# Re-measured durations in a kernel's instruction planner, and the order of all instructions searched anew

## The chip, the cores and the metric

The kernel runs on one core of a Trainium2 chip. The metric is the time of one execution on the device, in microseconds (us). Five engines work side by side, each through its own queue in order: PE (TensorE: matmuls and transposes, with its weight loads shown apart as PEld), DVE (VectorE), ACT (ScalarE), POOL (GpSimd) and SP (SyncE, which here only issues DMAs).

## What is computed

Two stages on a batch of 4, 8 heads, 768 steps and 48 channels per head, all in float32. The first is a recurrence per head:

```python
for t in range(S):
    cur = np.einsum('bhd,bhe->bhde', u[None] * kt, vt)
    y[:, :, t] = np.einsum('bhd,bhde->bhe', rt, state + cur)
    state = wt[:, :, :, None] * state + np.einsum('bhd,bhe->bhde', kt, vt)
```

The second takes y as x (4 x 768 x 384) through four attention experts of width 64. A gate picks two experts for each token; each expert is causal attention:

```python
    q = x @ wq[e];  k = x @ wk[e];  v = x @ wv[e]
    scores = scale * (q @ k.transpose(0, 2, 1))      # causal mask, then softmax
    ye = a @ v @ wo[e]
    out += mask[..., None] * w[:, :, kk:kk + 1] * ye   # the two picked experts
```

## The kernel before

The work is cut into 8 units (b, g): batch b, and half g of the sequence (384 steps). Each unit has a recurrence part, `rwkv`, and an attention part, `moe`, which needs the x of its own unit and, for g = 1, the K and V of both halves.

In `rwkv` the recurrence is done in chunks of 64 steps, six to a unit, for four pairs of heads p. The names in the rows are those of its tiles, and the digits behind a name are batch, half and pair. Two scans on DVE make the running products of the decay within each chunk, `suf` (L377) and `pre` (L381). Four elementwise products may stand on DVE or on POOL, as the planner chooses: `kt` (k by suf, L384), `mr` (r by pre, written over `pre`, L386), `uk` and `ur` (written over `nat`, L391 and L394). `rk` (L397) is a sum on DVE, `ux` (`xn`: for each head three small instructions on ACT, L404, or one on DVE or POOL, L406) starts the tile of y. PE transposes the keys (`ktp`, L414), makes the chunks' states (`ups`, L431), the products within a chunk (`aps`, L493, for two pairs at once) and the two parts of y (`yps`, L469 and L472). DVE carries the state from chunk to chunk by five or six instructions that depend on each other (`wst`, L440); a state scaled by the decay is `ys` (L450, DVE or POOL). DVE masks `aps` into `am` (L502) and adds `yps` to `xn` (L478). PE transposes y (`xp`, L519), ACT and DVE split it into a high and a low part (`xh` L521, `xl` L523).

In `moe` PE projects (`pp` L565 for Q and K, `vp` L588 for V and the gate), makes the scores (`sp`, L656 and L661), transposes the weights of the softmax (`tp`, L686), multiplies them by V (`yp`, L714) and projects out (`op`, L782). DVE finds each row's maximum (`mx`, L670), ACT takes the exponential (`a`, L672), and the copies out of PSUM (`ATa`, `ATb`, `kts`, `ob`, `v_sb`) stand on ACT (L226) or DVE (L228). Two banks of PSUM serve `rwkv` (`rw`), two `moe` (`mo`), and two double ones the scores (`sc`).

Nothing of the order is written by hand. `Plan.add` records each piece of work with its reads and writes, the engines that it may run on and its duration on each. `Plan.order` then plays the program through: at each step it takes, over all engines, the piece that could start first. On one engine it chooses among the pieces that could start within a slack of 125 ns by a due time, which is the stage's due time plus the entry of the table `WISH` for this kind of work and this unit. A change of PE's tiling costs `DRAIN`, a wait for another engine costs the entry of `WAITS`, and pieces in `BOTH` do not run on DVE and POOL at once. What comes out is the order of each engine's queue, the choice of engine and the buffer of each tile. The chip then runs these queues with semaphores; the planned times themselves are used nowhere.

PE's queue also holds 94 matmuls that compute nothing (`warm`, L832): 14 come first, and 80 are due last of all, so that they fill holes at the start.

## Time and profile before

| what | us |
|---|---|
| median of 3 runs (377.25 to 378.18) | 377.8 |
| the profiled execution | 380.95 |
| its span, first to last instruction | 379.2 |
| PE busy | 358.2 |
| DVE busy | 318.4 |
| ACT busy | 203.8 |
| POOL busy | 145.7 |

A row of the timeline gives start and duration of one instruction, or of several of a kind in a row, from the span's start. Matmuls overlap: on PE the start-to-start distance is the cost. An instruction's duration on the other engines also overlaps the next one's by a tenth of a microsecond where they don't depend on each other.

### The profile page before, as it was taken

What the parts mean: (1) busy time and instruction counts of PE and PEld (TensorE: products, weight loads), DVE (VectorE), ACT (ScalarE), POOL (GpSimd) and SP (SyncE); (2) the same over time, 40 slices, a digit from 0 to 9 for tenths busy, and PEclk for the clock granted to TensorE, in tenths of its full rate; (3) what the DMA queues carried; (4) which work ended last, traced back from release to release, by engine and by line L of the source; (5) the groups of instructions that cost most, each with busy time, mean ns of one, the idle gap of its engine ahead of it and who ended that gap; (6) DMA issues with size and microseconds to landing.
All of it is one profiled execution on the core that took longest, in us unless ns stands there. A gap on an engine that the chain in (4) does not pass through costs nothing.

```text
span 379.2 us, 12634 instructions
## 1 busy us (share of the span) xinstructions
PE 358.2 (94%) x5123; PEld 274.8 (72%) x5131; DVE 318.4 (84%) x800; ACT 203.8 (54%) x601; POOL 145.7 (38%) x262
## 2 busy tenths in 40 slices
PE   7889989999999999998899999999999999999996
PEld 2445777688867777776786867787887769977865
DVE  6999997988999999849997999997999965366863
ACT  3262325746666646736643654637764733376663
POOL 2758453735611536132571555833622010210010
PEclk9999999999999999999999999999999999999999
DMA  7877525353525354423374335454203001000101
GB/s 257 330 255 257 176 94 162 99 184 117 170 72 182 104 149 131 141 63 100 128 211 131 110 96 174 144 174 142 67 16 111 3 18 45 22 2 2 42 22 63
DMA packets 18058, 45.17 MB, mean 119 GB/s; under 512 B 2000, under 2 KB 9424, under 8 KB 18000
## 3 DMA queue, kind: packets, MB, share of 16 engines
q1 hardware_dynamic: 18000, 44.37, 36.1%
q8 instruction: 40, 0.66, 0.8%
q14 instruction: 18, 0.15, 0.1%
HBM read 39.64 MB, written 4.72 MB: 117 GB/s over the span
## 4 chain that ended last, share of the span: by engine, by line
PE 58%; DVE 25%; ACT 5%; issue 4%; DMA 2%; POOL 2%; ACTq 0%; DVEq 0%; POOLq 0%; SPq 0%
PE pp L565 9%; PE yp L714 8%; PE tp L686 8%; PE sp L656 7%; PE vp L588 5%; DVE mx L670 5%; PE op L782 5%; DVE wst L440 4%; DVE suf L377 3%; DVE am L502 3%; PE yps L472 3%; ACT a L672 3%; PE ups L431 2%; DMA nat<-in_nat_dram 2%; DVE pre L381 2%
## 5 line engine op out<-in xcount | busy, mean ns | idle before, releaser
L672 ACT ACTIVATE a<-sp,mx 128x128 f32<-128x128 f32 (+5 forms) x96 | 60.6, 635 | 32.1 <-DVE mx L670 31.2
L670 DVE TENSOR_REDUCE mx<-sp 128x1 f32<-128x128 f32 (+5 forms) x96 | 56.8, 617 | 6.9 <-PE sp L661 5.2
L686 PE MATMUL tp<-ident,a 128*128 128x128 f32 x336 | 56.5, 285 | 4.0 <-ACT a L672 1.6
L686 PEld LDWEIGHTS tp<-ident,a 128*128 128x128 f32 x336 | 37.0, 140 | 15.8 <-ACT a L672 5.1
L440 DVE SCALAR_TENSOR_TENSOR wst<-wst,suf,ups 112x48 f32<-112x48 f32 x160 | 41.5, 260 | 5.3 <-PE ups L431 1.2
L226 ACT COPY ATa<-tp 128x512 f32<-128x512 f32 (+3 forms) x70 | 33.6, 493 | 17.3 <-PE tp L686 16.8
L377 DVE TENSOR_TENSOR_SCAN suf<-lt,one_suf 128x390 f32<-128x390 f32 x32 | 34.4, 1076 | 3.5 <-DMA lt<-in_wkr_dram 1.7
L714 PE MATMUL yp<-ATa,v_sb 128*64 128x384 f32 (+2 forms) x240 | 37.2, 433 | 0.2 <-ACT ATa L226 0.2
L565 PE MATMUL pp<-xh,wh_qk 128*128 128x384 f32 x96 | 36.9, 384 | 0.2
L404 ACT ACTIVATE xn<-nat,rk 128x48 f32<-128x48 f32 x108 | 27.4, 324 | 17.5 <-DVE rk L397 17.4
L386 POOL TENSOR_TENSOR pre<-lt,pre 128x384 f32<-128x384 f32 x22 | 22.9, 1042 | 30.8 <-DVE pre L381 30.8
L450 POOL TENSOR_TENSOR ys<-wst,suf 112x240 f32<-112x240 f32 (+1 forms) x27 | 21.3, 790 | 34.5 <-DVE wst L440 20.7
L381 DVE TENSOR_TENSOR_SCAN pre<-lt,inv_pre 128x390 f32<-128x390 f32 x32 | 32.9, 1027 | 0.4
L565 PE MATMUL pp<-xh,wl_qk 128*128 128x384 f32 x96 | 32.7, 341 | 0.0
L565 PE MATMUL pp<-xl,wh_qk 128*128 128x384 f32 x96 | 32.7, 340 | 0.0
L472 PEld LDWEIGHTS yps<-ys,pre 64*64 64x64 f32 (+1 forms) x704 | 23.3, 136 | 12.7 <-issue 6.8
L472 PE MATMUL yps<-ys,pre 64*64 64x48 f32 (+1 forms) x704 | 28.2, 225 | 4.1 <-DVE am L502 1.8
L394 POOL TENSOR_TENSOR nat<-nat 128x288 f32<-128x288 f32 x28 | 24.2, 868 | 14.2 <-DVE nat L391 11.3
L391 POOL TENSOR_TENSOR nat<-nat,u_sb 128x288 f32<-128x288 f32 x23 | 21.4, 932 | 20.5 <-DMA nat<-in_nat_dram 11.8
L384 POOL TENSOR_TENSOR kt<-lt,suf 128x384 f32<-128x384 f32 x22 | 21.1, 961 | 20.2 <-DVE suf L377 15.9
L469 PE MATMUL yps<-vy,am 64*64 64x48 f32 x768 | 27.5, 223 | 0.0
L502 DVE TENSOR_TENSOR am<-aps,dec_mask 64x384 f32<-64x384 f32 (+1 forms) x48 | 26.4, 549 | 0.9
(129 smaller groups left out, 869.7 us busy)
## 6 DMA issues: line engine op xcount, KB each, us to landing
lt<-in_wkr_dram SPq DMA_DIRECT2D x31, 579.5 KB, 4.3
nat<-in_nat_dram SPq DMA_DIRECT2D x32, 432.0 KB, 3.5
vy<-in_vY_dram SPq DMA_DIRECT2D x32, 144.0 KB, 2.6
out_dram<-ob SPq DMA_DIRECT2D x24, 192.0 KB, 1.9
...
```

Source lines behind the costliest of these rows:

```text
L226: nc.scalar.copy(o, i)
L377: plan.add("suf", {"DVE": t_scan(WB)}, lambda e, suf=suf, w_=w_: nc.vector.tensor_tensor_scan(rev(suf()), rev(w_()), rev(one_suf), 0.0, op ...
L381: plan.add("pre", {"DVE": t_scan(WB)}, lambda e, pre=pre, w_=w_: nc.vector.tensor_tensor_scan(flat(pre()), w_()[:, 0:WB - 1], flat(inv_pre ...
L440: nc.vector.scalar_tensor_tensor(new, ws[0:112, c0 + c - 1, :], sfv()[0:112, c, 0:1], u()[0:112, o], op0=ALU.mult, op1=ALU.add)
L469: nc.tensor.matmul(yps[h]()[half(q), o], am()[half(h), c, :], vy()[half(h), c, :], start=zero, stop=i == 2)
L472: nc.tensor.matmul(yps[h]()[half(q), o], pre()[r, c, 0:C], ys()[r, c, :], start=i == 0, stop=False)
L502: nc.vector.tensor_tensor(am()[o], aps()[i, 0:NH * C].rearrange("p (c j) -> p c j", j=C), dec_mask[i, None, :].to_broadcast([i.stop - i.st ...
L565: nc.tensor.matmul(pp()[:, 0:384], w[:, qk, k, cs], x()[:, k, :], start=(k == j == 0), stop=(k == j == 2))
L670: plan.add("max", {"DVE": t_dve(n)}, lambda e, x=x, mx=mx: nc.vector.tensor_reduce(mx(), spv(x), axis=AX.XY, op=ALU.max, negate=True), [sp ...
L672: plan.add("exp", {"ACT": t_exp(n)}, lambda e, x=x, y=y, mx=mx, a=a: nc.scalar.activation(a()[:, 0:n].rearrange("p (a n) -> p a n", a=np_) ...
L686: nc.tensor.transpose(tp()[:, j * 128:(j + 1) * 128], a()[:, (j0 + j) * 128:(j0 + j + 1) * 128], ident)
L714: nc.tensor.matmul(yp()[e * 64:e * 64 + 64, lo:hi], v_sb[ep]()[:, j, e * 64:e * 64 + 64], at, start=(j == 0), stop=(j == nj - 1))
```

## The change

Durations that the planner is told are replaced, and the table of due times is a new one, found by searching anew with these durations. No arithmetic, no tile, no size and no number of buffers changes. The planner also looks at 40 instead of 24 candidates of each engine, and `ys`, which may stand on DVE or POOL before and now, costs 100 ns more on DVE. The rows of `WISH` (58 kinds of work by 8 units) are new but for entries that no work uses; two are shown.

```diff
 def t_pool(cols):
-    return 30 + 2.45 * cols
+    return 60 + 2.25 * cols
...
-         "ACT": dict(PE=164 + SAFE, DVE=143, ACT=127, POOL=170, SP=130), ...
+         "ACT": dict(PE=185 + SAFE, DVE=180, ACT=127, POOL=170, SP=130), ...
...
-    def order(self, free, slack=60.0, width=24):
+    def order(self, free, slack=60.0, width=40):
...
-                    plan.add("ws", {"DVE": 115}, grow, ...
+                    plan.add("ws", {"DVE": 172}, grow, ...
...
-            plan.add("ys", prod((NH - 1 + g) * D), scaled, ...
+            plan.add("ys", {"DVE": t_dve((NH - 1 + g) * D) + 100, "POOL": t_pool((NH - 1 + g) * D)}, scaled, ...
...
-                    plan.add("am", {"DVE": t_dve(384)}, mask, [apss[x]], [(am, h)])
+                    plan.add("am", {"DVE": 575 if x == 0 else 565}, mask, [apss[x]], [(am, h)])
...
-                plan.add("proj", {"PE": 3 * 172}, mm, ...
+                plan.add("proj", {"PE": 525}, mm, ...
...
-                plan.add("vproj", {"PE": 3 * 122}, mm, ...
+                plan.add("vproj", {"PE": 356}, mm, ...
...
-                plan.add("av", {"PE": 2 * 0.905 * (hi - lo) + 4}, mm,
+                plan.add("av", {"PE": 1.68 * (hi - lo) + 2}, mm,
...
-            plan.add("g3", {"DVE": 640}, over, ...
+            plan.add("g3", {"DVE": 530}, over, ...
...
-                plan.add("op", {"PE": 3 * 172}, mm, ...
+                plan.add("op", {"PE": 522}, mm, ...
...
-    am=[-523.53, -400.44, -469.75, -522.32, -432.29, -446.5, -350.6, -400.44],
+    am=[-301.84, -35.43, -160.17, -6.95, -164.62, -115.51, -12.82, -195.52],
...
-    uk=[-496.59, -240.01, 105.83, -310.53, -51.05, -237.91, 134.69, -17.82],
+    uk=[392.44, 446.59, 355.21, 364.53, 378.87, 449.7, 367.72, 367.15],
...
-T_APS, T_UPS, T_YPS = 1100, (395, 330), (816, 890)
-DRAIN = 100
-T_SC = (330, 500, 670, 850, 1040, 1210)
+T_APS, T_UPS, T_YPS = 763, (393, 380), (737, 750)
+DRAIN = 95
+T_SC = (490, 562, 745, 915, 1085, 1275)
```

Counted in the two programs: PE has the same matmuls in both, and changes its tiling 261 times before and 262 times now. All 94 `warm` stand ahead of the first projection (`pp0000`) in both. DVE has 24 instructions fewer, POOL 10 more and ACT 24 more:

| work | DVE before, now | POOL before, now | ACT before, now |
|---|---|---|---|
| `kt` | 10, 5 | 22, 27 | |
| `mr` (`pre`) | 10, 6 | 22, 26 | |
| `uk` (`nat`, L391) | 9, 2 | 23, 30 | |
| `ur` (`nat`, L394) | 4, 6 | 28, 26 | |
| `ys` | 5, 3 | 27, 29 | |
| `ux` (`xn`; three small ones on ACT stand for one of the others) | 10, 11 | 18, 12 | 108, 123 |
| copies `ATa` | 26, 15 | | 70, 81 |
| copies `ATb`, `kts`, `ob` | 14, 9, 5 before; 13, 8, 3 now | | 18, 23, 19 before; 19, 24, 21 now |
| copies `v_sb` | 1, 7 | | 47, 41 |

The first place is in the recurrence of unit (0, 1), while unit (0, 0) is projected. DVE's queue before, from the end of one state's chain (`wst`) to the mask `am` of the pairs 0 and 1, for which PE's `yps010` waits:

```order
L440 SCALAR_TENSOR_TENSOR wst1_81<-wst1_81,suf011_649,ups0110_740 112x48
L594 COPY lg00_775<-vp001_756 128x4
L377 SCALAR_TENSOR_TENSOR suf012_791<-lt012_483,one_suf_66 128x390
L377 SCALAR_TENSOR_TENSOR suf013_821<-lt013_510,one_suf_66 128x390
L502 TENSOR_TENSOR am010_830<-aps010_795,dec_mask_86 128x384
L502 TENSOR_TENSOR am011_836<-aps011_797,dec_mask_86 64x384 x2
```

And now:

```order
L577 TENSOR_TENSOR Kl00_775<-pp0001_729,Kh00_767 128x384
L440 SCALAR_TENSOR_TENSOR wst1_81<-wst1_81,suf011_584,ups0110_738 112x48
L440 SCALAR_TENSOR_TENSOR wst1_81<-wst1_81,suf011_584,ups0111_741 112x48
L440 SCALAR_TENSOR_TENSOR wst1_81<-wst1_81,suf011_584,ups0110_738 112x48
L381 SCALAR_TENSOR_TENSOR pre012_791<-lt012_404,inv_pre_69 128x390
L572 SCALAR_TENSOR_TENSOR Ql001_821<-pp0010_763,Qh001_788 128x384
L502 TENSOR_TENSOR am010_827<-aps010_795,dec_mask_86 128x384
L502 TENSOR_TENSOR am011_833<-aps011_797,dec_mask_86 64x384 x2
L577 TENSOR_TENSOR Kl01_854<-pp0011_784,Kh01_839 128x384
L397 TENSOR_REDUCE rk013_860<-nat013_720 128x6
L377 SCALAR_TENSOR_TENSOR suf013_895<-lt013_419,one_suf_66 128x390
```

The scan `suf013`, which stood directly ahead of the masks, now stands behind them; the scan `pre012` and a split of Q stand ahead.

POOL's queue at the same place before:

```order
L450 TENSOR_TENSOR ys010_738<-wst0_80,suf010_508 112x288
L394 TENSOR_TENSOR nat013_714<-nat013_714 128x288
L450 TENSOR_TENSOR ys011_793<-wst1_81,suf011_649 112x288
L384 TENSOR_TENSOR kt012_832<-lt012_483,suf012_791 128x384
L384 TENSOR_TENSOR kt013_842<-lt013_510,suf013_821 128x384
```

And now (`ys010` is on DVE):

```order
L391 TENSOR_TENSOR nat013_720<-nat013_720,u_sb_84 128x288
L384 TENSOR_TENSOR kt012_780<-lt012_404,suf012_761 128x384
L450 TENSOR_TENSOR ys011_793<-wst1_81,suf011_584 112x288
L394 TENSOR_TENSOR nat013_720<-nat013_720 128x288
L386 TENSOR_TENSOR pre012_791<-lt012_404,pre012_791 128x6x64
L391 TENSOR_TENSOR nat100_755<-nat100_755,u_sb_84 128x288
L394 TENSOR_TENSOR nat100_755<-nat100_755 128x288
L384 TENSOR_TENSOR kt013_913<-lt013_419,suf013_895 128x384
```

Between `kt012` and `kt013` POOL now has five other products.

The second place is in the recurrence of unit (2, 0). DVE's queue before, around the chain `wst2`, whose reads free the PSUM banks that PE's `yps201` then writes:

```order
L377 SCALAR_TENSOR_TENSOR suf203_3262<-lt203_2684,one_suf_66 128x390
L440 SCALAR_TENSOR_TENSOR wst2_82<-wst2_82,suf202_3101,ups2021_3248 112x48
L391 TENSOR_TENSOR nat210_3214<-nat210_3214,u_sb_84 128x288
L440 SCALAR_TENSOR_TENSOR wst2_82<-wst2_82,suf202_3101,ups2020_3245 112x48
L228 COPY ATb1101_3305<-tp11114_3279 128x128
L440 SCALAR_TENSOR_TENSOR wst2_82<-wst2_82,suf202_3101,ups2021_3248 112x48
L379 RECIPROCAL inv_pre_69<-suf203_3262 128x6
L440 SCALAR_TENSOR_TENSOR wst2_82<-wst2_82,suf202_3101,ups2020_3245 112x48
L440 SCALAR_TENSOR_TENSOR wst2_82<-wst2_82,suf202_3101,ups2021_3248 112x48
```

And now:

```order
L478 TENSOR_TENSOR xn20_2485<-yps2010_3204,xn20_2485 128x3x48
L478 TENSOR_TENSOR xn20_2485<-yps2011_3206,xn20_2485 128x3x48
L228 COPY wst2_82<-ups2020_3248 112x48
L440 SCALAR_TENSOR_TENSOR wst2_82<-wst2_82,suf202_2922,ups2021_3251 112x48
L440 SCALAR_TENSOR_TENSOR wst2_82<-wst2_82,suf202_2922,ups2020_3248 112x48
L440 SCALAR_TENSOR_TENSOR wst2_82<-wst2_82,suf202_2922,ups2021_3251 112x48
L440 SCALAR_TENSOR_TENSOR wst2_82<-wst2_82,suf202_2922,ups2020_3248 112x48
L440 SCALAR_TENSOR_TENSOR wst2_82<-wst2_82,suf202_2922,ups2021_3251 112x48
```

The chain now stands behind the additions of `yps201`, without other work inside it. Over the whole program a `wst` directly follows another one 80 times now and 70 times before, of 160.

## Rows read from the trace of the kernel before

**Rows 1.** Busy time of each engine over the span, its share, and its instructions (the page's first part).

```profile
PE 358.2 (94%) x5123; PEld 274.8 (72%) x5131; DVE 318.4 (84%) x800; ACT 203.8 (54%) x601; POOL 145.7 (38%) x262
```

**Rows 2.** Busy time by stage: the stretch, its length, then busy time and instructions of PE, PEld, DVE, ACT and POOL, PE's granted clock, the DMA engines' share and GB/s.

```profile
0.00:42.00 42.00, 35.65 (x480) 18.78 (x489) 36.86 (x86) 15.92 (x48) 23.89 (x37) 1.00 0.74 260
42.00:60.00 18.00, 16.35 (x253) 14.43 (x251) 15.58 (x41) 4.56 (x16) 10.04 (x16) 0.91 0.40 129
60.00:300.00 240.00, 230.56 (x3522) 181.52 (x3522) 217.84 (x554) 140.99 (x421) 103.79 (x173) 1.00 0.40 125
300.00:360.00 60.00, 59.88 (x736) 48.38 (x735) 38.99 (x99) 32.53 (x94) 6.28 (x27) 1.00 0.06 21
360.00:379.20 19.20, 15.74 (x140) 11.73 (x138) 9.16 (x24) 9.80 (x24) 1.71 (x9) 1.00 0.12 42
```

**Rows 3.** The same by stage for the instructions on the tile `warm` alone: PE's busy time and instructions.

```profile
0.00:42.00 42.00, 24.57 (x86) 1.00 0.74 260
```

**Rows 4.** Pieces of the chain of work that ended last, in order of time: start, length, engine, tile, line and number of matmuls.

```profile
83.22 0.86 PE aps L493 x48
...
162.93 3.17 PE pp L565 x18
...
292.45 3.38 PE yp L714 x24
...
322.49 4.33 PE vp L588 x36
```

**Rows 5.** The timeline at the first place, of PE, DVE and POOL: start, duration, engine, line, operation, tiles, shape; in brackets the engine's idle time before it and what ended it.

```profile
48.51 0.96 DVE L377 TENSOR_TENSOR_SCAN suf<-lt,one_suf 128x390 f32<-128x390 f32 x1
48.60 1.34 POOL L450 TENSOR_TENSOR ys<-wst,suf 112x288 f32<-112x288 f32 x1
48.66 0.93 PE L493 MATMUL aps<-pre,kt 64*64 64x64 f32 x48
...
49.90 0.96 POOL L384 TENSOR_TENSOR kt<-lt,suf 128x384 f32<-128x384 f32 x1
49.97 1.72 DVE L377 TENSOR_TENSOR_SCAN suf<-lt,one_suf 128x390 f32<-128x390 f32 x1 [0.51 <-POOL ys L450]
...
51.38 0.34 PE L565 MATMUL pp<-xl,wh_qk 128*128 128x384 f32 x1
51.61 1.68 DVE L502 TENSOR_TENSOR am<-aps,dec_mask 128x384 f32<-128x384 f32 x3
...
52.28 0.32 PE L472 MATMUL yps<-ys,pre 64*64 64x48 f32 x4 [0.56 <-DVE am L502]
...
53.44 0.26 PE L472 MATMUL yps<-ys,pre 48*64 48x48 f32 x2 [0.83 <-DVE am L502]
```

**Rows 6.** The timeline at the second place, of DVE, POOL and PE.

```profile
182.26 0.24 DVE L440 SCALAR_TENSOR_TENSOR wst<-wst,suf,ups 112x48 f32<-112x48 f32 x1
182.49 1.23 DVE L391 TENSOR_TENSOR nat<-nat,u_sb 128x288 f32<-128x288 f32 x1
...
184.30 0.57 DVE L440 SCALAR_TENSOR_TENSOR wst<-wst,suf,ups 112x48 f32<-112x48 f32 x2
...
182.43 0.98 POOL L384 TENSOR_TENSOR kt<-lt,suf 128x384 f32<-128x384 f32 x1 [1.08 <-DVE suf L377]
...
183.37 0.29 PE L661 MATMUL sp<-causal,idh 64*128 64x128 bf16 x4
184.71 0.28 PE L472 MATMUL yps<-ys,pre 64*64 64x48 f32 x2 [1.06 <-POOL nat L394]
```

**Rows 7.** Groups of instructions of work that changes its engine: line, engine, operation, tiles, shape, number, busy time, mean ns of one, then idle time of the engine before them.

```profile
L384 DVE TENSOR_TENSOR kt<-lt,suf 128x384 f32<-128x384 f32 x10 | 6.4, 644 | 0.1
L386 DVE TENSOR_TENSOR pre<-lt,pre 128x384 f32<-128x384 f32 x10 | 6.2, 616 | 0.1
L391 DVE TENSOR_TENSOR nat<-nat,u_sb 128x288 f32<-128x288 f32 x9 | 6.0, 664 | 0.5 <-DMA nat<-in_nat_dram 0.5
L450 DVE TENSOR_TENSOR ys<-wst,suf 112x288 f32<-112x288 f32 (+1 forms) x5 | 2.2, 446 | 0.1
L228 DVE COPY ATa<-tp 128x512 f32<-128x512 f32 (+3 forms) x26 | 13.0, 510 | 4.5 <-PE tp L686 4.2
L394 DVE TENSOR_TENSOR nat<-nat 128x288 f32<-128x288 f32 x4 | 2.4, 602 | 0.0
L228 DVE COPY v_sb<-vp 128x128 f32<-128x128 f32 x1 | 0.3, 280 | 0.0
L384 POOL TENSOR_TENSOR kt<-lt,suf 128x384 f32<-128x384 f32 x22 | 21.1, 961 | 20.2 <-DVE suf L377 15.9 <-PE tp L686 4.2
L391 POOL TENSOR_TENSOR nat<-nat,u_sb 128x288 f32<-128x288 f32 x23 | 21.4, 932 | 20.5 <-DMA nat<-in_nat_dram 11.8 <-ACT ATa L226 7.7 <-PE sp L661 0.5
```

**Rows 8.** The same for the two scans and the chain of states, which stay on DVE.

```profile
L377 DVE TENSOR_TENSOR_SCAN suf<-lt,one_suf 128x390 f32<-128x390 f32 x32 | 34.4, 1076 | 3.5 <-DMA lt<-in_wkr_dram 1.7 <-POOL ys L450 1.5
L381 DVE TENSOR_TENSOR_SCAN pre<-lt,inv_pre 128x390 f32<-128x390 f32 x32 | 32.9, 1027 | 0.4
L440 DVE SCALAR_TENSOR_TENSOR wst<-wst,suf,ups 112x48 f32<-112x48 f32 x160 | 41.5, 260 | 5.3 <-PE ups L431 1.2 <-ACT wst L226 1.2
```

**Rows 9.** The timeline at 43.8 us: five instructions of one chain of states in a row.

```profile
43.80 1.46 DVE L440 SCALAR_TENSOR_TENSOR wst<-wst,suf,ups 112x48 f32<-112x48 f32 x5
```

**Rows 10.** Busy time by stage, the stretch in which the granted clock was low for a part.

```profile
40.00:60.00 20.00, 17.80 (x261) 15.44 (x261) 17.43 (x46) 5.81 (x20) 11.30 (x18) 0.91 0.43 133
```

**Rows 11.** Who waited for whom in 60 to 300 us, of the weight loads and of DVE: total us, times, longest.

```profile
PEld tp L686 <- ACT a L672: 4.7, 10, 1.0
PEld yps L472 <- issue: 3.6, 12, 0.7
PEld xp L519 <- DVE xn L478: 2.3, 5, 0.9
DVE kts L228 <- PE ktp L414: 1.8, 2, 1.2
DVE mx L670 <- PE sp L661: 1.8, 4, 0.8
```

More of the change, by code (lines that the diff above doesn't have):

```diff
@@ L67 @@
 WAITS = {"PE": dict(PE=0, DVE=215, ACT=215, POOL=260, SP=200), "DVE": dict(PE=139 + SAFE, DVE=127, ACT=128, POOL=164, SP=130),
-         "ACT": dict(PE=164 + SAFE, DVE=143, ACT=127, POOL=170, SP=130), "POOL": dict(PE=150 + SAFE, DVE=140, ACT=150, POOL=128, SP=130),
+         "ACT": dict(PE=185 + SAFE, DVE=180, ACT=127, POOL=170, SP=130), "POOL": dict(PE=150 + SAFE, DVE=140, ACT=150, POOL=128, SP=130),
          "SP": dict(PE=2000, DVE=2000, ACT=2000, POOL=2000, SP=2000)}
@@ L443, in rwkv @@
                 if c0 + c:
-                    plan.add("ws", {"DVE": 115}, grow, [ups[a], suf, kw + (c0 + c - 1,)], [kw + (c0 + c,)])
+                    plan.add("ws", {"DVE": 172}, grow, [ups[a], suf, kw + (c0 + c - 1,)], [kw + (c0 + c,)])
                 else:
@@ L451, in scaled @@
                                     sfv()[0:112, o, 0:1].to_broadcast([112, NH - 1 + g, D]), op=ALU.mult)
-            plan.add("ys", prod((NH - 1 + g) * D), scaled, [suf] + [kw + (c0 - g + c,) for c in range(NH - 1 + g)], [ys])
+            plan.add("ys", {"DVE": t_dve((NH - 1 + g) * D) + 100, "POOL": t_pool((NH - 1 + g) * D)}, scaled, [suf] + [kw + (c0 - g + c,) for c in range(NH - 1 + g)], [ys])
             def finish(p=p, n=n, pre=pre, am=am, ys=ys, vy=vy):
@@ L566, in mm @@
                                          stop=(k == j == 2))
-                plan.add("proj", {"PE": 3 * 172}, mm, [(x_, kk) for x_ in (xh, xl) for kk in range(3)] + [("wh", "qk", qk), ("wl", "qk", qk)] + ([pp] if k else []), [pp],
+                plan.add("proj", {"PE": 525}, mm, [(x_, kk) for x_ in (xh, xl) for kk in range(3)] + [("wh", "qk", qk), ("wl", "qk", qk)] + ([pp] if k else []), [pp],
                          claim=(K if qk else Q)[ep])
@@ L588, in mm @@
                         nc.tensor.matmul(vp()[:, 0:260], x()[:, k, o], w[:, k, :], start=(k == j == 0), stop=(k == j == 2))
-                plan.add("vproj", {"PE": 3 * 122}, mm, [(x_, kk) for x_ in (xh, xl) for kk in range(3)] + [("wh", "vg", 0), ("wl", "vg", 0)] + ([vp] if k else []), [vp],
+                plan.add("vproj", {"PE": 356}, mm, [(x_, kk) for x_ in (xh, xl) for kk in range(3)] + [("wh", "vg", 0), ("wl", "vg", 0)] + ([vp] if k else []), [vp],
                          claim=v_sb)
@@ L734, in over @@
                 nc.vector.tensor_tensor(gg()[:, t], gg()[:, t], ge()[:, t], op=ALU.mult)
-            plan.add("g3", {"DVE": 640}, over, [(asum, i, x) for i in range(i0, i1) for x in range(E)] + [ge, gs], [gg])
+            plan.add("g3", {"DVE": 530}, over, [(asum, i, x) for i in range(i0, i1) for x in range(E)] + [ge, gs], [gg])
             def parts(e):
@@ L782, in mm @@
                         nc.tensor.matmul(op()[:, 0:DM], y()[:, t], w[:, ep, :], start=(j + ep == 0), stop=(j == 2 and ep == 1))
-                plan.add("op", {"PE": 3 * 172}, mm, [(y, i0) for pair in parts for y in pair] + [("wh", "o", 0), ("wl", "o", 0)] + ([op] if ep else []), [op])
+                plan.add("op", {"PE": 522}, mm, [(y, i0) for pair in parts for y in pair] + [("wh", "o", 0), ("wl", "o", 0)] + ([op] if ep else []), [op])
             ob = sb([128, DM], F32, "ob", f"ob{n0}{i}")
@@ new lines @@
+    lg=[-1.62, -118.83, 59.05, 21.84, 6.25, -0.16, 34.74, -39.0],
+    masks=[-161.79, -23.07, -23.07, -23.07, -23.07, -23.07, -23.07, -23.07],
+    masks2=[79.83, 0.0, 0.0, 0.0, 0.0, 0.0, 0.0, 0.0],
+    max=[19.71, 79.7, -23.04, -72.57, 204.08, -33.32, -5.24, -30.67],
+    mr=[110.74, 106.99, 19.11, 199.62, 180.1, 182.75, 177.95, 181.63],
+    ob=[43.59, -95.35, -92.73, 44.24, -39.18, -124.86, -18.15, -91.2],
+    op=[23.3, -0.98, -0.01, 122.4, 10.98, -1.63, 73.5, -54.88],
+    pre=[-169.29, -164.82, -144.47, 68.03, -160.45, -7.52, -87.21, 308.37],
@@ new lines @@
+    warm=[-194.2, 7.19, 7.19, 7.19, 7.19, 7.19, 7.19, 7.19],
+    wload=[-157.46, 30.67, 30.67, 30.67, 30.67, 30.67, 30.67, 30.67],
+    ws=[-369.75, -75.13, -127.49, -133.07, -107.43, -151.0, -53.7, -375.64],
+    wso=[134.04, 0.0, 0.0, 0.0, 0.0, 0.0, 0.0, 0.0],
+    wsqk=[34.68, 0.0, 0.0, 0.0, 0.0, 0.0, 0.0, 0.0],
+    wsvg=[-70.16, 0.0, 0.0, 0.0, 0.0, 0.0, 0.0, 0.0],
+    xh=[-12.37, -56.29, -22.87, -10.39, -36.35, 69.75, 132.03, -100.52],
+    xl=[-430.45, -236.59, -441.96, -440.47, -445.56, -346.71, -211.52, -341.26],
@@ new lines @@
+    xp=[24.83, -74.44, -68.9, -4.5, -5.92, -3.51, -33.12, -90.73],
+    y=[-87.34, -73.4, -175.91, -159.11, -161.51, -67.98, 76.95, -50.73],
+    yh=[-124.07, -33.32, -122.6, -94.33, -118.02, -122.1, -26.96, -123.19],
+    yl=[45.27, 45.46, 32.82, 102.12, 93.22, 62.97, 24.72, 133.22],
+    yps=[-188.07, -89.71, -225.66, -100.97, -184.2, -254.38, -164.13, -123.04],
+    yr=[-163.57, -221.26, -230.6, -149.41, 92.05, -222.88, -360.35, -162.48],
+    ys=[149.8, 232.43, 259.4, 152.07, 227.16, 233.47, 224.45, 209.68],
+)
```

89 lines of the change are left out of this document (33 added, 56 removed).

## The prediction

> **What bounds the kernel now.** I read the busy times first. PE is busy for 94% of the span and DVE for 84% [rows 1]; the reader should not stop there, since PE's time holds work that computes nothing. Next come the stages [rows 2]. Up to 42 us the first unit's recurrence runs on DVE and POOL, and 24.57 us of PE's time there are `warm` fillers [rows 3]: DVE with what it waits for bounds this stage. From 42 to 300 us PE and DVE are both nearly full. PE stands idle for 1.65 us of 18 and 9.44 us of 240, and DVE is busy for 217.84 of 240, 91%. From 300 to 360 us no recurrence is left but a little, DVE falls to 38.99 of 60, 65%, and PE idles 0.12 us. From 360 us the last unit drains through short dependent steps. So PE's work sets the time from 42 to 360 us, and what can be gained there is PE's holes. These lie where DVE is crowded.
>
> The third view is who waits in the middle stage [rows 11], and there is no one big wait: the holes are many and mostly under 1 us. A modelled matmul also ends later than the next could start, so a hole shows shorter than it is: the second place has a last score matmul at 183.37 us with a recorded end at 183.66, and the next matmul at 184.71 [rows 6]. The idle of 9.44 us is therefore a lower bound of the holes. I put the rest at up to 6 us, an estimate: some 40 waits of PE and its weight loads times the 0.15 us by which a record outlasts the slot of a matmul (`aps`: 48 take 0.93 us to the last recorded end and 0.86 us on the chain, and a single `pp` is recorded at 0.34 us while 18 take 3.17, 0.176 each) [rows 4, 5].
>
> Last I read two holes closely, because they show how a plan goes wrong. At 49.97 us the scan of pair 3 runs beside POOL's `kt` and takes 1.72 us, where the scan before it took 0.96; the masks `am` stand behind it in DVE's queue, and PE, which has run out of projections at 51.7 us, waits for them twice [rows 5]. At 182.49 us a product `nat` takes 1.23 us beside `kt` (the mean of its kind is 0.66 [rows 7]), it stands inside a chain of states, and `yps` starts 1.06 us late [rows 6].
>
> **The change, its truth.** The new durations fit this trace where I can look. `aps` runs 0.86 us on the chain [rows 4], which is the new 763 + 95 ns and not the old 1100 + 100. Three matmuls of `pp` take 3.17 / 6 = 0.528 us against 525 now and 516 before. The 24 of `yp` take 3.38 us, and the new formula gives 1.68 x 1920 columns + 12 + 95 = 3.33 us, the old one 3.60. `vp` takes 4.33 / 12 = 0.361 us against 356 and 366. A step of the chain of states advances by 0.30 us [rows 9]; the new price of 172 plus DVE's 127 to itself is 299, the old one 242. Over 160 steps the old plan was some 9 us short of DVE's real work, and on 48 masks of 0.56 us (1.68 / 3 [rows 5]) planned at 465 ns some 5 us. So the old search filled DVE beyond what it holds, in the very stage where DVE is at 91%. Some prices stay wrong: a scan of 391 columns is still planned at 882 ns and has means of 1076 and 1027 [rows 8], and POOL's `kt` is planned at 924 now (971 before) and takes 961, its `nat` at 708 and takes 932 [rows 7].
>
> **The change, load.** By counts of the two programs and the means of [rows 7], DVE loses 5 x 0.644 (`kt`) + 4 x 0.616 (`mr`) + 7 x 0.664 (`uk`) + 2 x 0.446 (`ys`) + 11 x 0.510 (`ATa`) = 16.8 us, and gains 2 x 0.602 (`ur`) + 6 x 0.280 (`v_sb`) = 2.9 us. The other copies and `xn`, four off and one on, taken like `ATa`, are 1.5 us off. Ten more steps of the chains follow directly on their own chain, at 0.30 instead of the 0.23 us when another instruction comes between [rows 6, 9]: 0.7 us on. Together 14.7 us leave DVE, 5% of its work. POOL takes some 12 us and ACT some 10; both are far from full (38% and 54% [rows 1]), so that alone costs nothing while nobody waits for them.
>
> **The change, stage by stage.** PE's instructions and its 261 and 262 changes of tiling are the same, so PE's own work changes by nothing.
>
> 0 to 42 us: all 94 fillers stay ahead of the first projection, and DVE has about the same list ahead of the third `xl` (73 rows then, 70 now). `kt` of the first pair moves to POOL, 0.961 for 0.644 us, and POOL has more products there, each of which can stretch a scan. I take +0.5 us, between -1 and +3 (four scans of the unit stretched by 0.76 us, 1.72 less 0.96).
>
> 42 to 60 us: between `aps` and the masks two scans are replaced by one scan, three chain steps and a split of Q, and `suf013`, with its stretch, comes behind the masks. PE in turn has no more than projections and V ahead of `yps010`. The holes of 0.56 and 0.83 us should close. The granted clock was 0.91 in 40 to 60 us [rows 10] and 1.00 in all other stages: with levels of full and half speed that is 3.6 us at half speed, right after the holes, and some 1.8 us lost. If the holes close, the clock has no reason to fall. Together at most 3.4 us; since `pre012` may be stretched by `ys011` beside it, I take -2.5, between -3.4 and 0.
>
> 60 to 300 us: 9.4 us of holes shown, up to 6 more hidden. By load alone little would come: from 65% to 91% of DVE the idle share of PE goes from 0.2% to 3.9% [rows 2], so at 86% (12 of the 14.7 us off 217.84) it would be near 3.2%, some 1.8 us less. The rest must come from the distances: with chain steps, masks and matmuls priced as they are, the search can put a consumer behind its producer where the old one guessed. At the second place `uk` has left the chain, which now stands behind `yps201`. I take -6, between 0 and -13.
>
> 360 us to the end: both queues end in the same transposes, the last two `yp` groups and `op`; DVE's last copies stand in another order. 0, between -1 and +1.
>
> The sum is +0.5 - 2.5 - 6 = -8.0 us. On the profiled execution of 380.95 us (span 379.2) that gives 372.95. That execution lies 3.15 us above the median of the runs, so the median becomes 377.8 - 8.0 = 369.8 us.
>
> **The rivals.** *The freed time is lost at the memory that DVE and POOL share (slower).* A scan took 1.72 instead of 0.96 us beside `kt`, and `nat` 1.23 [rows 5, 6]. Eighteen products move to POOL (5 `kt`, 4 `mr`, 7 `uk`, 2 `ys`). If each stretches a DVE instruction by 0.76 us, 13.7 us come back on DVE, of the 14.7 that left. The products on POOL are also each 0.3 us longer (0.961 for 0.644), and 8 of them end on PE's way: 2.4 us. With DVE's load as before, the waits as many, and that delay on top: 377.8 + 2.4 = 380.2 us. It decides when the stretch per moved product passes some 0.65 us. Against it: the mean scan is 1.05 us, 0.09 above the free one, with 140 products on POOL already [rows 8], so the planner's rule of keeping the two apart works mostly. The Trainium skill has a rule that says the same as this rival: Perfetto Trace Analysis, section "Optimizing Scalar/DVE Operations", reminds that the two share a read port of SBUF, so that offloading between them might not help; SBUF — State Buffer, section "SBUF: two separate sides", calls it an exclusive lock held for a whole instruction. By that rule the trace agrees in kind (the 1.72 us scan), and the sum would be the 380.2 us of this rival; by the mean rows it would stay near 370.
>
> *The holes only change their place.* What is still misjudged (scans by 0.15 to 0.19 us, 64 of them; POOL by up to 0.22) makes as many small waits as before, and only the place at 50 us and the load's 1.8 us count: -2.5 - 1.8 + 0.5 + 1.5 of new holes gives 375.5 us. For it: the many short waits of [rows 11]. Against it: the chains and masks alone were 14 us wrong.
>
> *Nothing to be measured.* Gains and losses cancel: 377.8 us.
>
> **How the numbers follow.** A difference of under 0.3%, 1.1 us, can't be told from no change here. Forecast, 361 to 374 us: 0.70. Holes in other places, 374 to 376.7: 0.12. Nothing: 0.07. Slower, mostly by the shared memory: 0.11. So faster is 0.82. The most that the rows allow is -1 - 3.4 - 13 - 1, which gives 359.4 us; the range runs from 361 to 377.5, leaves out the slower case and the last of the gains, and takes in the second rival.
>
> **What would show it.** If right: DVE near 304 us busy, POOL near 157; PE's idle time in 42 to 60 us under 0.7 us with a granted clock of 1.00, and in 60 to 300 us under 6 us; 0 to 42 us within 1 us; the scans' means still below 1.1 us. If the mean of the scans rises to 1.2 us or more and PE idles as before, it was the first rival. If DVE's time falls as counted and PE's idle in 60 to 300 us stays at 8 us or more, it was the second. It would be wrong altogether if the first projection came later than 45 us or the clock fell in a new place.

## The result and the profile after

| | before | after |
|---|---|---|
| median of the runs, us | 377.78 (4 runs) | 367.57 (366.65 to 369.6, 4 runs) |
| the profiled execution, us | 380.95 | 367.91 |
| its span, us | 379.2 | 366.1 |

The ratio is 0.9738, with a 95% interval of 0.9695 to 0.9781: 10.2 us faster by the medians, where 8.0 were forecast. Between the two profiled executions it is 13.0 us, and most of the 2.8 us between these two differences lies in the profile of before, which was longer than most executions (below).

The first part of the page of after answers to [rows 1]:

```profile
PE 350.2 (96%) x5124; PEld 272.3 (74%) x5131; DVE 307.3 (84%) x776; ACT 211.6 (58%) x625; POOL 158.0 (43%) x272
```

DVE is at 307.3 us (304 forecast) and POOL at 158.0 (157). PE computes the same matmuls and shows 350.2 us busy where it showed 358.2: part of PE's "busy" time before was waiting, and 1.7 us of it came of a stretch at half clock. Busy time by stage of after (stretch, its length, busy time and instructions of PE, PEld, DVE, ACT and POOL, granted clock, DMA share, GB/s), against [rows 2]:

```profile
0.00:42.00 42.00, 34.69 (x479) 18.11 (x486) 36.19 (x81) 15.75 (x47) 23.35 (x36) 1.00 0.78 269
42.00:60.00 18.00, 16.87 (x296) 15.27 (x298) 16.20 (x46) 9.27 (x33) 11.17 (x16) 1.00 0.49 144
60.00:300.00 240.00, 236.38 (x3711) 188.00 (x3701) 215.91 (x549) 149.02 (x445) 115.40 (x190) 1.00 0.40 123
300.00:347.00 47.00, 46.57 (x530) 39.34 (x529) 31.91 (x82) 28.66 (x83) 6.37 (x23) 1.00 0.05 18
347.00:366.10 19.10, 15.68 (x130) 11.63 (x128) 7.14 (x23) 8.87 (x21) 1.70 (x9) 0.98 0.15 52
```

PE's idle time in 60 to 300 us falls from 9.44 to 3.62 us, in 42 to 60 us from 1.65 to 1.13, and the clock there is 1.00 instead of 0.91. The last 19 us are as before (15.68 busy of 19.1, 15.74 of 19.2). In 0 to 42 us PE idles 7.31 us instead of 6.35, and the first projection begins at 43.4 us instead of 42.1. The 1.13 us of the next stage are the end of the wait just ahead of it, up to 43.13 us; behind that no idle time of PE is shown up to 60 us:

```profile
43.13 0.52 PE L414 MATMUL ktp<-ident,kt 128*128 128x128 f32 x3 [1.46 <-DVE xl L523]
```

The timeline of after at the first place, against [rows 5]:

```profile
49.99 0.96 DVE L381 TENSOR_TENSOR_SCAN pre<-lt,inv_pre 128x390 f32<-128x390 f32 x1
50.15 1.27 POOL L450 TENSOR_TENSOR ys<-wst,suf 112x288 f32<-112x288 f32 x1 [0.20 <-DVE wst L440]
...
51.31 1.70 DVE L502 TENSOR_TENSOR am<-aps,dec_mask 128x384 f32<-128x384 f32 x3
...
53.72 0.33 PE L472 MATMUL yps<-ys,pre 64*64 64x48 f32 x8
53.88 0.96 DVE L377 TENSOR_TENSOR_SCAN suf<-lt,one_suf 128x390 f32<-128x390 f32 x1
```

The masks end at 53.01 us, `yps` starts at 53.72 with no idle time ahead of it, and `suf013` is late for nobody. Nor is the scan `pre012` stretched: `ys`, which began after it, took 1.27 us. The scans of after, against [rows 8]:

```profile
L381 DVE TENSOR_TENSOR_SCAN pre<-lt,inv_pre 128x390 f32<-128x390 f32 x32 | 35.1, 1096 | 0.2
L377 DVE TENSOR_TENSOR_SCAN suf<-lt,one_suf 128x390 f32<-128x390 f32 x32 | 33.0, 1033 | 3.2 <-DMA lt<-in_wkr_dram 1.7 <-POOL ys L450 1.3
```

Their means, 1.096 and 1.033 us, stay below the 1.2 us that would have spoken for the shared memory.

### The profile page after: what moved, and what is told of

It reads as the page before. It is cut to its first block, busy times and chain, and to the rows that moved or that the text cites. A ratio compares the mean times of both kernels' runs of the same rounds, so it can differ in the third digit from the quotient of the medians.

```text
span 366.1 us, 12622 instructions
## 1 busy us (share of the span) xinstructions
PE 350.2 (96%) x5124; PEld 272.3 (74%) x5131; DVE 307.3 (84%) x776; ACT 211.6 (58%) x625; POOL 158.0 (43%) x272
## 4 chain that ended last, share of the span: by engine, by line
PE 74%; DVE 14%; DMA 5%; ACT 3%; issue 2%; SPq 1%; DVEq 0%; ACTq 0%
PE pp L565 13%; PE tp L686 10%; PE yp L714 9%; PE sp L656 8%; PE vp L588 7%; PE op L782 7%; PE ups L431 3%; PE yps L472 3%; DVE mx L670 3%; PE aps L493 3%; DMA w_vg<-in_wvg_dram 2%; PE ktp L414 2%; PE yps L469 2%; PE xp L519 2%; DMA lt<-in_wkr_dram 2%
## 5 line engine op out<-in xcount | busy, mean ns | idle before, releaser
L686 PE MATMUL tp<-ident,a 128*128 128x128 f32 x336 | 54.9, 283 | 1.5 <-ACT a L672 0.7
L226 ACT COPY ATa<-tp 128x512 f32<-128x512 f32 (+3 forms) x81 | 38.9, 491 | 19.3 <-PE tp L686 18.4
L384 POOL TENSOR_TENSOR kt<-lt,suf 128x384 f32<-128x384 f32 x27 | 28.0, 1038 | 36.5 <-DVE suf L377 36.5
L404 ACT ACTIVATE xn<-nat,rk 128x48 f32<-128x48 f32 x123 | 30.8, 325 | 15.7 <-DVE rk L397 15.7
L391 POOL TENSOR_TENSOR nat<-nat,u_sb 128x288 f32<-128x288 f32 x30 | 28.0, 936 | 17.9 <-DMA nat<-in_nat_dram 11.7
L377 DVE TENSOR_TENSOR_SCAN suf<-lt,one_suf 128x390 f32<-128x390 f32 x32 | 33.0, 1033 | 3.2 <-DMA lt<-in_wkr_dram 1.7
L381 DVE TENSOR_TENSOR_SCAN pre<-lt,inv_pre 128x390 f32<-128x390 f32 x32 | 35.1, 1096 | 0.2
L502 DVE TENSOR_TENSOR am<-aps,dec_mask 64x384 f32<-64x384 f32 (+1 forms) x48 | 26.4, 551 | 1.2 <-PE aps L493 0.2
L832 PE MATMUL warm<-one_suf 128*128 128x512 bf16 x87 | 24.4, 417 | 2.4 <-POOL one_suf L246 1.4
L472 PEld LDWEIGHTS yps<-ys,pre 64*64 64x64 f32 (+1 forms) x704 | 21.1, 133 | 7.1 <-issue 3.3
L656 PE MATMUL sp<-Kh,Qh 64*128 64x384 f32 (+4 forms) x128 | 25.6, 389 | 0.1
```

The source lines that it names most:

```text
L226: nc.scalar.copy(o, i)
L377: plan.add("suf", {"DVE": t_scan(WB)}, lambda e, suf=suf, w_=w_: nc.vector.tensor_tensor_scan(rev(suf()), rev(w_()), rev(one_suf), 0.0, op ...
L381: plan.add("pre", {"DVE": t_scan(WB)}, lambda e, pre=pre, w_=w_: nc.vector.tensor_tensor_scan(flat(pre()), w_()[:, 0:WB - 1], flat(inv_pre ...
L472: nc.tensor.matmul(yps[h]()[half(q), o], pre()[r, c, 0:C], ys()[r, c, :], start=i == 0, stop=False)
L656: nc.tensor.matmul(spv(x)[:, h, :], q()[p, t], flat(k())[p, o], start=j == 0, stop=j == 2 and h < np_ - 1)
L686: nc.tensor.transpose(tp()[:, j * 128:(j + 1) * 128], a()[:, (j0 + j) * 128:(j0 + j + 1) * 128], ident)
```

## Experiments

The theory at the start was that of the prediction: two separate gains, load taken off DVE and better distances between producer and consumer, each of which could be had alone. The rivals were that one half carries all of it, and that a single misplaced operation makes each hole.

**1 and 2: the engines alone and the order alone.** A string of one letter for each piece of work overrides the engine at emission; the order of emission stays that of the kernel's own planner. `engines_alone` is before with after's engines, `order_alone` after with before's.

```diff
+EN = dict(D="DVE", A="ACT", P="POOL", E="PE", S="SP")
+ENGINE_OF = ("ADSEEEE...")
-        o["fn"](o["e"])
+        o["fn"](EN[ENGINE_OF[o["n"]]])
```

> The queues in the order of the kernel before, with every one of the 146 pieces of work that change their engine on the engine of the changed kernel: the load moves alone. If distances are what counts (the theory), only the load's own share comes, some 1.8 us: 376. If the load is what counts (rival), most of the gain of 10.2 us comes: 370 or less. If the memory that DVE and POOL share takes it back (rival), it is slower than before, 380, with mean scans over 1.15 us.

> The queues in the order of the changed kernel, with the engines of the kernel before for the same 146 pieces: the order moves alone. By the theory PE's idle time in 60 to 300 us falls most of the way from 9.4 to 3.6 us and the time is near 371. If the load is what counts, DVE is as full as before and the time stays at 375 or more.

Measured: 395.81 us, ratio 1.0425 (1.0403 to 1.0447), and 391.81 us, ratio 1.0305 (1.0269 to 1.0342). Neither time that the theory expected (376 and 371 us) came. Each half alone is slower than before by more than the two together gain. In the first, PE's waits (total us, times, longest) are headed by the masks, 5.6 us where before's profile has 1.8; that they now stand behind work that was never planned ahead of them is the likely reason, which these rows don't show. The scans' means of 1.148 and 1.045 us stay below the 1.15 of the shared-memory rival:

```profile
PE yps L472 <- DVE am L502: 5.6, 9, 0.9
```

In the second the granted clock falls in five stretches, 20.5 us at half speed together; the stage of 42 to 60 us:

```profile
42.00:60.00 18.00, 15.13 (x205) 13.31 (x200) 14.62 (x33) 6.43 (x19) 10.50 (x12) 0.81 0.39 115
```

So the two are one plan. This choice of engines loses without the order made for it, this order loses without its engines, and the forecast's split into load and distances can't be had by halves.

**3 and 4: the scan ahead of the masks.** In before `suf013` is moved behind the masks; in after it is moved ahead of them.

```diff
+    suf, am = of["suf"][7], of["am"][6:9]
+    todo.remove(suf)
+    todo.insert(todo.index(am[2]) + 1, suf)   # scan_behind; in scan_ahead: todo.index(am[0])
```

> The kernel before with one instruction moved: the scan suf013 stands behind the masks of pairs 0 and 1 of unit (0, 1) instead of ahead of them. By the theory the two holes of 0.56 and 0.83 us ahead of yps close and the granted clock stays at 1.00 in 40 to 60 us: 375.3, 2.5 us less. If a hole only changes its place (rival), kt013 comes 1.7 us later, PE waits for it in ktp013, and the time stays within 1 us of 377.8.

> The changed kernel with the same scan put back directly ahead of the masks. By the theory the masks end 0.9 us later than now, yps010, which follows them by under 1 us, waits 0.5 to 0.9 us, and the time is 368.3 (0.7 more). If the clock falls after that hole as it did in the kernel before, it is 370. If a hole only changes its place, 367.6.

Measured: `scan_behind` 378.06 us against 379.84, ratio 0.9963 (0.9946 to 0.9981), some 1.4 to 1.8 us and less than the 2.5 of the forecast. The two holes ahead of `yps010` (0.56 and 0.83 us) are gone, but 3 us later a hole of 0.85 us opens ahead of the next pair's `yps`, so more than half of them only changed its place:

```profile
55.20 0.38 PE L472 MATMUL yps<-ys,pre 64*64 64x48 f32 x6 [0.85 <-POOL c L618]
```

The clock is 1.00 throughout, and the granted clock of the other executions says more than this one profile. It is 0.999 or more over the span in all 11 of `scan_behind`; of the 16 of before beside them, 6 have 0.995 or 0.996, as the profile of before has with its 3.4 us at half speed. Those 6 take 380.26 us in the mean, the other 10 379.35.

`scan_ahead` 372.28 us, ratio 0.9801 (0.9767 to 0.9834): by the ratios of after (here and in 8) some 2.4 to 3.1 us lost by one scan, more than any of the expected times allowed. Its timeline:

```profile
50.19 0.80 POOL L394 TENSOR_TENSOR nat<-nat 128x288 f32<-128x288 f32 x1
50.26 3.18 DVE L377 TENSOR_TENSOR_SCAN suf<-lt,one_suf 128x390 f32<-128x390 f32 x1
...
50.95 0.91 POOL L386 TENSOR_TENSOR pre<-lt,pre 128x384 f32<-128x384 f32 x1
51.82 0.79 POOL L391 TENSOR_TENSOR nat<-nat,u_sb 128x288 f32<-128x288 f32 x1
52.69 1.34 POOL L394 TENSOR_TENSOR nat<-nat 128x288 f32<-128x288 f32 x1
53.36 1.68 DVE L502 TENSOR_TENSOR am<-aps,dec_mask 128x384 f32<-128x384 f32 x3
...
54.03 0.87 PE L414 MATMUL ktp<-ident,kt 128*128 128x128 f32 x3 [2.49 <-POOL nat L394]
```

The scan begins 0.07 us after a product on POOL and ends only when three of them, each starting as the last ends, are over: 3.18 us instead of 0.96. The fourth product takes 1.34 us instead of 0.80. PE stands idle for 2.49 us, not ahead of `yps010` as expected but ahead of the transposes `ktp`. These read nothing of the `nat` that the profile names: they write one of the two `rw` banks, which hold `aps` until the masks have read it, and they begin 0.1 us after the first of the three masks ends (53.36 us and a third of 1.68). From 53.63 us, still inside this hole, the clock is at half speed for 6.8 us; in the stage from 42 to 60 us it is 0.82. Over the span it is 0.985 to 0.995 in five of the six executions:

```profile
42.00:60.00 18.00, 15.51 (x202) 13.86 (x204) 14.98 (x33) 6.08 (x21) 8.46 (x10) 0.82 0.37 119
```

**5: the product inside the chain of states.** The second place, in before alone: `uk` of `nat210` goes behind the last step.

```diff
+    uk = of["uk"][20]
+    todo.remove(uk)
+    todo.insert(todo.index(of["ws"][94]) + 1, uk)
```

> Before with one product of 128x288 on DVE (uk of nat210), which stands inside a chain of wst steps at 184 us and holds up the yps behind it, put behind the last step of that chain. The theory that each hole of the middle stage is a DVE operation in the wrong place by itself expects the 1.06 us hole gone and the time 0.7 to 1.1 us below before (ratio 0.997 to 0.998). The rival, that a hole closed alone opens another further on, because PE then comes earlier to the next piece that DVE has not made, expects the idle PE time of 60 to 300 us within 0.4 us of before's 9.44 and the ratio within 0.9985 to 1.001.

Measured: 378.58 us, ratio 1.000 (0.9986 to 1.0013). The expected gain is not there. PE's idle time in 60 to 300 us is 7.26 us in its profile, so the rival's 9.44 isn't there either, though its ratio is. A reason is in the trace of `scan_behind`, where this product still stands inside the chain:

```profile
180.37 0.45 DVE L391 TENSOR_TENSOR nat<-nat,u_sb 128x288 f32<-128x288 f32 x1
180.38 1.27 POOL L384 TENSOR_TENSOR kt<-lt,suf 128x384 f32<-128x384 f32 x1 [1.08 <-DMA nat<-in_nat_dram]
...
181.82 0.52 PE L472 MATMUL yps<-ys,pre 64*64 64x48 f32 x3 [0.20 <-DVE wst L440]
```

Here DVE's product began 0.01 us ahead of POOL's `kt`, took 0.45 us, and `kt` waited (1.27 us). In the profile of before it began 0.06 us behind `kt` and took 1.23 us [rows 6]. A few hundredths of a microsecond decide who waits. With the product in the same place the wait of `yps` is 1.06 us in one profile and 0.20 in the other, so it can't be priced from one of them; how often it is long is not shown. The Trainium skill (SBUF — State Buffer, section "SBUF: two separate sides") calls the shared ports an exclusive lock that whoever starts first holds for a whole instruction; both traces agree with it.

**6 and 7: the start of the program.** `vg_later` puts the two casts of `w_vg` behind the third `xl`; `vg_warm` also has six fillers more ahead of the `ktp` before the first projection.

```diff
+    for o in of["wsvg"]:
+        todo.remove(o)
+    at = todo.index(of["xl"][2]) + 1
+    todo[at:at] = of["wsvg"]
+    todo[at:at] = 6 * [of["warm"][0]]   # vg_warm alone; there at = the place of that ktp
```

> After with the two casts of the v and gate weights (wh_vg on ACT, wl_vg on DVE) taken out of the two queues ahead of the first unit's chain and put behind its third xl. The theory that the prologue's loss of 1.3 us (first projection at 43.4 us, before 42.1) is ACT and DVE standing behind a weight transfer that lands 9.05 us after its issue expects the first projection at 41.5 to 42.5 us, the wait of ups for kts (1.3 us) gone, and some 366.5 us. The rival, that the prologue is long because the scans and masks of DVE beside POOL's kt are (1.54 for suf003, 1.98 for pre010), expects the first projection to stay at 43 to 43.5 us and 367.6. If the casts, now behind, stand in the way of the first vp, the stage from 42 to 60 us gets more idle PE time by 1 us or more and the time is over 368.

> The version with the later v and gate casts, and six warm-up matmuls more ahead of the kt transpose that stands before the first projection. The theory that this version lost its 1.4 us of the prologue to the half clock of 43.3 to 46.7 us, and that the clock fell since PE had sat idle for 1.46 us before it, expects the clock at full speed from 42 to 60 us, the first projection at 42.0 us and 1.3 to 1.7 us less than that version: some 366.5 us, ratio to before 0.968. The rival, that the clock falls in some executions whatever stands there, expects the same time as without (ratio 0.9715) and a stretch at half speed again. If the six warm-ups themselves are late (they take 1.3 us), the first projection moves to 42.5 us or later.

Measured: 368.41 us, ratio 0.9715 (0.9694 to 0.9737), and 368.81 us, ratio 0.9744 (0.9703 to 0.9785). First projections at 42.0 and 42.3 us as expected; `vg_later` has half clock from 43.3 to 46.7 us, `vg_warm` none in its profile. But two of the five other executions of `vg_warm` have a granted clock of 0.995, and its time is no better: the fillers are not shown to keep the clock up. Neither version is faster than after.

**8: after again**, unchanged, on the chip of `vg_warm` and `dve_load`.

> After unchanged, on the same chip as the others of this call, so that versions that differ from it by a microsecond can be set against it: ratio to before 0.970 to 0.978. The first projection at 43.4 us within 0.3. If the stretches at half clock are a matter of single executions, its profile may show one now; if they follow from the order alone, it shows none before 360 us.

Measured: 368.2 us, ratio 0.9719 (0.9689 to 0.975). The first projection is at 42.2 us, not 43.4: `w_vg` landed 6.3 us after its issue, in the first profile 9.0. The theory that after's own order loses 1.3 us there falls, but the transfer is only part of it. The later landing had put DVE's work back by 0.44 us at the first chain of states and by 0.77 when the scan `pre010` began; then this scan took 1.98 us in the first profile and 0.98 in the second. In the first it began behind POOL's `ys`, in the second ahead of it, and there `ys` was the longer one. The first profile of after, then `after_again`:

```profile
32.72 0.60 POOL L450 TENSOR_TENSOR ys<-wst,suf 112x240 f32<-112x240 f32 x1
32.91 1.98 DVE L381 TENSOR_TENSOR_SCAN pre<-lt,inv_pre 128x390 f32<-128x390 f32 x1
```

```profile
32.15 0.98 DVE L381 TENSOR_TENSOR_SCAN pre<-lt,inv_pre 128x390 f32<-128x390 f32 x1
32.26 1.26 POOL L450 TENSOR_TENSOR ys<-wst,suf 112x240 f32<-112x240 f32 x1
```

The hole of 1.46 us ahead of `ktp` is in both profiles of after and in `vg_later`, and only in the last did the clock fall behind it. Of the ten executions of after, here and in the result, four have a granted clock of 0.991 or 0.995 over the span. They take 368.96 us in the mean, the other six 367.26. Where in them the clock fell isn't on record.

**9: the load put back.** 32 fills that nobody reads.

```diff
+        n += o["e"] == "DVE"
+        if o["e"] == "DVE" and 130 <= n < 610 and n % 15 == 0:
+            nc.vector.memset(idle, 0.0)
```

> After with 32 fills of a 128x390 tile that nobody reads (0.38 us each, 12.3 us in all), one behind every 15th instruction of DVE from the 130th to the 610th, so that DVE has about the busy time of before again, and the order is that of after. The theory that the load taken off DVE is what shortened the middle stage expects most of the gain gone: 373 to 377 us, idle PE time of 60 to 300 us at 8 or more. The rival, that the order's distances did it and DVE's idle time of some 24 us in that stage takes up the fills, expects 368 to 371 us and at most 2.5 us more of idle PE time than after's 3.62.

Measured: 370.63 us, ratio 0.9787 (0.9756 to 0.9818), 2.4 us over `after_again`. By stage, `dve_load`:

```profile
60.00:300.00 240.00, 234.07 (x3652) 186.83 (x3650) 219.12 (x570) 147.19 (x436) 113.32 (x187) 1.00 0.39 121
```

DVE is as full as before (219.12 us, 217.84 in [rows 2]), and PE idles 5.93 us against 3.80 in `after_again`. 2.4 us for 12.3 us of load is 0.2 for one; by this the 10 to 15 us that left DVE are worth 2 to 3 us of the 10. That is an estimate: the six executions of `after_again` lie 2 us apart, and a fill reads nothing and is spread evenly, unlike the work that left. The rest is the order, with the engines that it was made for.

**10 to 12: new tables by a short search**, with after's durations once and with before's twice; only `WISH` is replaced.

```diff
-WISH = dict(
...
+WISH = dict(   # 58 kinds by 8 units, from another search
...
```

> After's durations with a table of due times of another search: 7967 steps from before's table with each entry moved by up to 3 ns, whose plan was worth 367.9 us then and 356.6 us at the end (after's own table is worth 343.5 us by the same count, before's with its own durations 350.3). What counts here is the span less the planned end: 21.7 and 22.6 us in the two profiles of after, 25.8 to 28.9 us in those of before and of before with one piece moved. The theory that the new durations make the chip follow the plan more closely, whatever the table, expects 22 us within 2 here, a span of some 379 us and a time of 380.5. The rival, that the closer plan of after is luck of that one table, expects 24 to 28 as with the old durations, a time of 382 to 387.

> Before's durations with a table found by the same search, of 9063 steps (375.1 us planned at its start, 358.8 at its end). The theory that the old durations are what makes the chip fall behind the plan expects the span 26 to 29 us above the planned end, some 386 us, and a time of 387. The rival expects no more excess than with the new durations, 22 to 24 us, and a time of 383 or 384.

> Before's durations with a second table of the same search with other chances, of 8638 steps (375.1 us planned at its start, 360.9 at its end). The theory expects the span 26 to 29 us above the planned end, and a time of 388 to 391; the rival 22 to 24 us, and a time of 384 to 387. If the two tables with old durations differ from each other by more than 4 us in this excess, three tables can't tell the two apart.

Measured: 389.98 us, ratio 1.0293 (1.0252 to 1.0333); 386.99 (of the three executions that the ratio goes by; a fourth took 390.49), ratio 1.0186 (1.013 to 1.0243); 390.05, ratio 1.0284 (1.0225 to 1.0343). The spans exceed the planned ends by 31.2 (387.8 - 356.6), 26.4 (385.2 - 358.8) and 28.1 us (389.0 - 360.9). The theory wanted 22 for the first, and this falls. `new_prices` runs most of one stage at half clock and idles less in the next; its rows, and behind them the middle stage of `old_prices_1` and of `old_prices_2`:

```profile
42.00:60.00 18.00, 14.87 (x243) 13.11 (x244) 13.88 (x33) 4.20 (x15) 8.10 (x10) 0.62 0.50 164
60.00:300.00 240.00, 230.70 (x3592) 181.67 (x3592) 215.65 (x540) 140.60 (x423) 107.74 (x183) 1.00 0.39 122
```

```profile
60.00:300.00 240.00, 228.93 (x3479) 180.33 (x3479) 212.18 (x532) 138.35 (x417) 104.55 (x167) 0.98 0.38 121
```

```profile
60.00:300.00 240.00, 227.41 (x3517) 178.24 (x3516) 211.36 (x528) 138.18 (x423) 105.45 (x175) 1.00 0.39 124
```

By the granted clock, `new_prices` spends 17.1 us at half speed, the others 10.2 and 6.8; less half of that the excess is 22.7, 21.3 and 24.7 us. So it isn't shown that the new durations as such make the chip follow the plan. PE idles 9.30 us in the middle stage with the new ones and 11.07 and 12.59 with the old, which points their way, but from one table against two.

No version here is shown to beat after.

## Why the prediction was right

**The profile of before was a long execution.** It lies 3.15 us above the median, and two things in it cost time that most executions don't spend. The stretch at half clock (some 1.7 us) is in neither profile of before with one piece moved. By the granted clock of 0.995 or 0.996 over the span, 13 of the 51 executions of before beside the experiments have such a fall, on one chip none of 17; on the other three chips they take 0.9 to 1.3 us more than the rest. And the hole of 1.06 us depends on who began first. A pair without either is `uk_behind` (profiled at 377.86 us) and `after_again` (367.02): 10.8 us. Their busy times on the pages, `uk_behind` first:

```profile
PE 356.6 (95%) x5131; PEld 273.3 (73%) x5131; DVE 317.6 (84%) x800; ACT 203.6 (54%) x601; POOL 146.5 (39%) x262
```

```profile
PE 350.2 (96%) x5124; PEld 273.0 (75%) x5131; DVE 307.7 (84%) x776; ACT 211.6 (58%) x625; POOL 159.0 (44%) x272
```

The spans differ by 10.9 us (376.1, 365.2). Of these 6.4 are PE time shown as busy (356.6 - 350.2), and 4.5 are shown idle time (19.5 - 15.0).

**0 to 42 us, +0.5 forecast.** 1.3 us in one profile and 0.1 in the other. Right within its bounds. What moved it is a DMA's landing time and one stretched scan (8), 1.98 us for 0.98, of the kind that the upper bound was made from.

**42 to 60 us, -2.5.** The mechanism was right in part: with the scan behind the masks the two holes close and no execution loses the clock (3), and with it ahead of them, in after's order, a larger hole opens and most executions lose it (4). The size was too large: `scan_behind` measured 1.4 to 1.8 us. A hole of 0.85 us opened further on, and the 1.8 us of clock were counted as if every execution of before lost them. That the clock has no reason to fall once these holes close is not borne out: 13 of 51 executions of before have a fall and 4 of 10 of after, so on the medians the clock gave the change nothing. Nor does it always fall behind them: in the profile of `uk_behind` the same two holes (0.57 and 0.84 us) stand and the clock is 1.00. PE's idle time in the stage, forecast under 0.7, is 1.13 and, in `after_again`, 0.31 us.

**60 to 300 us, -6 of 0 to -13.** This term was too small. With the one before it, too large, it made the sum come near; that is luck, and the range had room for both. The shown idle alone fell by 5.8 us between the two profiles, by 3.5 in the clean pair (7.26 to 3.80), and the hidden part, which I had put at up to 6 us and for which the -6 left little room, came whole: 6.4 us over the span (PE's busy time, 356.6 to 350.2). Where it sat can be read from two groups of PE and the ACT group that feeds one of them (line, engine, operation, tiles, shape, number, busy time, mean ns, then idle time ahead and its releasers), `uk_behind`:

```profile
L672 ACT ACTIVATE a<-sp,mx 128x128 f32<-128x128 f32 (+5 forms) x96 | 60.6, 635 | 32.1 <-DVE mx L670 31.4 <-DVE gg L731 0.6
L686 PE MATMUL tp<-ident,a 128*128 128x128 f32 x336 | 56.6, 285 | 4.4 <-ACT a L672 1.5 <-DVE Ql L572 0.7 <-ACT ATa L226 0.5
L472 PE MATMUL yps<-ys,pre 64*64 64x48 f32 (+1 forms) x704 | 27.8, 222 | 2.7 <-DVE am L502 1.8 <-DVE ys L450 0.3 <-DVE xn L478 0.2
```

and `after_again`:

```profile
L672 ACT ACTIVATE a<-sp,mx 128x128 f32<-128x128 f32 (+5 forms) x96 | 60.7, 636 | 20.7 <-DVE mx L670 18.2 <-PE yps L469 1.1 <-PE vp L588 0.4
L686 PE MATMUL tp<-ident,a 128*128 128x128 f32 x336 | 55.0, 283 | 1.3 <-DVE am L502 0.5 <-DVE gT L749 0.4 <-ACT a L672 0.3
L472 PE MATMUL yps<-ys,pre 64*64 64x48 f32 (+1 forms) x704 | 26.0, 223 | 0.6 <-DVE wst L440 0.3 <-DVE xn L478 0.2
```

PE waits for the softmax `a`, ACT waits for the row maximum `mx` of DVE. ACT's wait falls from 31.4 to 18.2 us; the transposes lose 3.1 us of shown idle time, `yps`, which waited for the masks, 2.1. Their busy columns (1.6 and 1.8 us less) add up records that overlap and can't be set against the 6.4. From start to start they can: in the two traces the time from the start of the matmul ahead to that of each `tp` falls from 52.6 to 46.0 us over the span, that to each `yps` of L472 from 23.6 to 18.9, and that to all other matmuls together rises by 0.3. I had read the holes as those of the recurrence's chains and masks; more than half of what closed, 6.6 of 10.8 us, lies at the transposes. With the load put back (9; its lines stand one further down) the two are 47.6 and 20.1 us, and ACT's wait for `mx` is still only 21.3 us:

```profile
L673 ACT ACTIVATE a<-sp,mx 128x128 f32<-128x128 f32 (+5 forms) x96 | 60.8, 636 | 23.3 <-DVE mx L671 21.3 <-PE yps L470 1.1 <-PE aps L494 0.3
```

so what closed there comes mainly from the order of the queues and not from DVE's load. Which piece of the order does it, the place of `mx` in DVE's queue being the likely one, was not tried alone. The forecast's 1.8 us for load alone was near (2 to 3).

**360 us to the end, 0.** Right by the two profiles.

**DVE's count.** 14.7 us were to leave, and DVE's busy time fell by 11.1 us between the two profiles and by 9.9 in the clean pair. By sums of durations the work that moved takes 15.5 and 15.1 us less, and it was counted at 15.4. The work that stayed takes 1.2 and 2.5 us more, among it the two scans 0.8 and 0.6 and `yl` (L771) 1.0 and 1.6: so much comes back on DVE, as the first rival said; it asked for 13.7. The other 3.2 and 2.7 us are overlap: the forecast took whole durations, of which each overlaps the next by about a tenth of a microsecond, and there are 24 instructions fewer. The wait that this rival rests on is real. (4) shows its price where POOL's products stand in a row, (8) one of 1.0 us in after's own order; but the scans' means in the two profiles of after (1.096 and 1.033, 1.067 and 1.046 us) say that it stays small on the whole (0.96 undisturbed).

**The cause that I named, truer durations, is not shown.** The plan as a whole is shown (1, 2), and its worth by load and by order (9). Whether the same effort of search with the old durations would have found a plan as good stays open: three short searches (10 to 12) gave poorer plans of both kinds. Nor were the 40 candidates in place of 24 and the 100 ns on `ys` tried apart from the durations.
